# RetNet attention with a mixture-of-depths block on one core: twelve steps load k once and turn it on TensorE

## The chip, the core and the metric

The kernel runs on 1 core of one Trainium2 chip. The metric is the device time of one execution, in microseconds, as the median of the timed runs. The engines that appear below are TensorE (PE for its matmuls, PEld for its weight loads), VectorE (DVE), ScalarE (ACT), GpSimd (POOL) and SyncE (SP), whose queue issues nearly all transfers.

## The reference

Attention of the retention kind, for 8 batches, 8 heads, 576 positions and a head size of 64, all in float32:

```python
scores = scale * np.matmul(q, k.transpose(0, 1, 3, 2))
Dmat = np.where(rel >= 0, gamma[:, None, None] ** rel[None, :, :], 0.0)
ret = scores * Dmat[None, :, :, :]
return np.matmul(ret, v).astype(np.float32)
```

The result is regrouped to x with 8 x 576 rows of 512. Then, for each batch, the 128 rows with the largest score x·w_gate are taken, sent through a two-layer network (512 to 1024, ReLU, 1024 to 512), scaled by the sigmoid of their score and added to the row; the other rows stay as they are.

## The kernel before

**Attention by chunks.** The 576 positions of a batch are 9 chunks of 64. A step s takes two chunks, so the 8 batches make 36 steps; batch 0 is steps 0 to 4, with its ninth chunk in step 4. Half of the heads lie on partitions 0 to 63, the other half on 64 to 127, so matmuls of 64x64 run in pairs. For each step the host has packed a row of 2048 float32 a partition: q turned (head size on the partitions), k turned, v natural (positions on the partitions) and k natural. One transfer of 1 MB, `load`, brings them into a tile `raw` (8 buffers).

In step s TensorE makes, in `diagonal(s)`:
- u, the sum of k^T v over the chunks so far (`summed`): it takes k natural as the stationary operand and `vs`, v scaled by the decay, which POOL makes as soon as raw is there (`scaled`, 128x512);
- sc, the scores within a chunk: k turned against q turned.

and for the step before, in `crosswise(s - 1)`: y, from the masked scores am times vs, plus q turned times the state st of the chunk before. The generator `matmuls` takes two matmuls from each of the two lists in turn, so a step is about 16 such groups; the dictionary `inner` hangs further work in front of a given group. ACT copies u to st (`state`). `masked` multiplies sc by the causal mask on DVE. `values` scales y to xs: on ACT, in eight pieces of 128x64, for the steps in `BUSY`, and otherwise in one DVE instruction. `scored` makes the gate scores, `stored` writes xs out.

**Choice of rows and network.** `flatten`, `spread`, `compare` and `one_hot` find the rank of each row on DVE, with small matmuls in between; `fetch` gathers the chosen rows from the output by an indirect transfer of POOL (`xr`); `turn`, `up` and `down` are the network on TensorE (xg, h, ye). The pieces of the network of a batch are spread over the steps that follow its attention.

**What sets the order.** The order on each engine is the order of the program. Loads are put in it by `pe`: it counts TensorE's instructions (a float32 matmul is four, a transpose two), and at each edge of 256, where TensorE fetches its next block of instructions, it starts weights that are due (the list `due`, by step) and then raw loads, if fewer than 4 (in steps 4 to 6: 5) are ahead of the step. These transfers wait for the TensorE instruction at the edge. They go in order through the SP queue, together with the stores, which stand at the end of the steps that the dictionary `stores` names. A transfer in the queue that has to wait holds up all that is behind it.

For the prediction: "load s" is the load of step s, "vs(s)" the POOL instruction made from it, and "lead" the number of TensorE instructions between the edge that starts a load and the beginning of its step.

Of the kernel before, what the change touches and what calls it, by code (L numbers as in the profile page):

```python
# [10 lines left out]
F32 = mybir.dt.float32  # L11
# [6 lines left out]
P = 128  # L18
TINY = 2.0**-125
C = 64  # L20
# [19 lines left out]
def kernel(  # L40
# [37 lines left out]
    col = layout(NC, HG, cap)  # L78

    const = ctx.enter_context(tc.tile_pool(name="const", bufs=1))  # L80
    loads = ctx.enter_context(tc.tile_pool(name="loads", bufs=8))
    work = ctx.enter_context(tc.tile_pool(name="work", bufs=3))
    psum = ctx.enter_context(tc.tile_pool(name="psum", bufs=2, space=PSUM))

    def bank(name, tag="mm", bufs=3):
        return psum.tile([P, 512], F32, tag=tag, bufs=bufs, name=name)

    halves = [slice(0, C), slice(C, P)]

# [6 lines left out]
    raw, weights = {}, deque()  # L96
    now = {"at": BEFORE, "edge": BLOCK, "load": 0, "step": 0, "quiet": 0}

    def load(behind=None):
        s, now["load"] = now["load"], now["load"] + 1  # L100
        raw[s] = x = loads.tile([P, 4, DM], F32, name="raw")
        n = 4 if s else 2
        for a in range(0, 4, n):
            start(x[:, a : a + n, :],
                  qkvk[s, :, DM * a : DM * (a + n)].rearrange("p (a e) -> p a e", a=n), behind)

    def start(out, in_, behind):
        ins = nc.sync.dma_start(out=out, in_=in_)  # L108
        if behind is not None:
            tc.add_manual_dep(ins.ins, behind.ins.name, mybir.DependencyInfo(  # L110
                mybir.DependencyClass.Sync, mybir.DependencyReason.DATA), reason="behind a fetch")

    def pe(ins, n=4):

        now["at"] += n
        if now["at"] >= now["edge"] + SURE:
            now["edge"] += BLOCK
            lead = now["load"] - now["step"]
            if now["quiet"] and lead > 2:
                now["quiet"] -= 1  # L120
                return ins
            for _ in range(1 + (now["step"] > 8)):
                if weights and weights[0][0] <= now["step"]:
                    start(*weights.popleft()[1:], ins)

            ranks = (NC - 1) // 2 <= now["step"] < (NC - 1) // 2 + 3
            for _ in range(1 + (now["step"] == (NC - 1) // 2)):
                if now["load"] < NS and now["load"] - now["step"] < 4 + ranks:
                    load(ins)
        return ins  # L130
# [5 lines left out]
    def matmul(out, lhsT, rhs, **more):  # L136
        return pe(nc.tensor.matmul(out, lhsT, rhs, **more), 4 if lhsT.dtype == F32 else 2)  # L137
# [9 lines left out]
    load()  # L147
    w1_sb = const.tile([P, KD, F], F32, name="w1_sb")
    w2_sb = const.tile([P, FB, DM], F32, name="w2_sb")
    due = 5, 6, 8, 9, 9, 10, 10, 11  # L150
    assert FB == 8
    for i in range(FB // 2):
        e = slice(2 * P * i, 2 * P * i + 2 * P)
# [10 lines left out]
    eye = table[:, col["eye"] : col["eye"] + P]  # L164
# [5 lines left out]
    for _ in range(3):  # L170
# [7 lines left out]

    BUSY = range(1, (NC - 1) // 2 + 3)
    vs, am, sc_ps, y_ps, u_ps, st, xs, sc = {}, {}, {}, {}, {}, {}, {}, {}
    factor = lambda s, i: dec[:, i, chunk(s, 0)[1] : chunk(s, 0)[1] + 2, :].unsqueeze(3).to_broadcast(
        [P, 2, HG, D])

    def scaled(s):
        vs[s] = work.tile([P, DM], F32, name="vs", bufs=4)
        nc.gpsimd.tensor_tensor(out=four(vs[s]), in0=four(raw[s][:, 2, :]), in1=factor(s, 0),  # L188
                                op=OP.mult)

    def summed(s, a):

        b, c = chunk(s, a)
        if c == NC - 1:
            return
        if c == 0:
            u_ps[b] = bank("u_ps", "u", 1)
        for h in range(HG):
            for half in halves:
                yield lambda h=h, half=half: matmul(  # L200
                    u_ps[b][half, hd[0][h]], raw[s][half, 3, hd[a][h]], vs[s][half, hd[a][h]],
                    start=c == 0 and h == 0, stop=c == NC - 2, skip_group_check=True)
        state(s, a)

# [5 lines left out]
    def diagonal(s):  # L210

        if s:
            yield from summed(s, 0)
        sc_ps[s] = bank("sc_ps", "sc", 2)
        for a in range(2):
            for h in range(HG):
                for half in halves:
                    yield lambda a=a, h=h, half=half: matmul(
                        sc_ps[s][half, hd[a][h]], raw[s][half, 1, hd[a][h]],
                        raw[s][half, 0, hd[a][h]], start=True, stop=True, skip_group_check=True)  # L220
        masked(s)
        if s == 0:
            yield from summed(s, 0)
        yield from summed(s, 1)

    def crosswise(s):

        y_ps[s] = bank("y_ps", "y", 2)
        for a in range(2):
            for h in range(HG):  # L230
                for i, half in enumerate(halves):
                    yield lambda a=a, h=h, i=i, half=half: matmul(
                        y_ps[s][halves[1 - i], hd[a][h]], am[s][half, HG * a + h, :],
                        vs[s][half, hd[a][h]], start=a == 0 and h == 0, stop=chunk(s, a)[1] == 0,
                        skip_group_check=True)
        for a in range(2):
            b, c = chunk(s, a)
            if c == 0:
                continue
            for h in range(HG):  # L240
                for i, half in enumerate(halves):
                    yield lambda a=a, b=b, c=c, h=h, i=i, half=half: matmul(
                        y_ps[s][halves[1 - i], hd[a][h]], raw[s][half, 0, hd[a][h]],
                        st[b, c - 1][half, hd[0][h]], start=False, stop=True,
                        skip_group_check=True)

# [48 lines left out]
    def stored(s):  # L295
        (b, c), (b1, _) = chunk(s, 0), chunk(s, 1)
        for i, half in enumerate(halves):
            e = slice(W * i, W * i + W)
            if b == b1:
                nc.sync.dma_start(  # L300
                    out=outs[b][C * c : C * c + P, e].rearrange("(a t) e -> t a e", a=2),
                    in_=xs[s][half, :].rearrange("p (a e) -> p a e", a=2))
                continue
            nc.sync.dma_start(out=outs[b][C * c :, e], in_=xs[s][half, :W])
            nc.sync.dma_start(out=outs[b1][:C, e], in_=xs[s][half, W:])
# [128 lines left out]
    inner, first, soon, mid, late, then, ready, parts = {}, {}, {}, {}, {}, {}, [], deque()  # L434
# [11 lines left out]
    def plan(when, s, f, *a):  # L446
        when.setdefault(s, []).append((f, a))

    for b in range(B):
        end = cuts(b)  # L450
# [13 lines left out]
        s = there[-1]  # L464
# [28 lines left out]
        if b < B - 2:  # L493
# [3 lines left out]


    FETCH = (NC - 1) // 2 + 3
    stores = {4: [], 5: [0, 1, 2, 3], 6: [], FETCH: [], FETCH + 1: [], FETCH + 2: [5, 6],  # L500
              FETCH + 3: [7, 8], FETCH + 4: [9]}
    assert NC == 9
    scaled(0)
    scaled(1)
    for s in range(NS + 1):
        now["step"] = s
        now["at"] += 1.5
        if s == FETCH + 1:
# [109 lines left out]
```

## Time and profile before

| | |
|---|---|
| Time, median of 3 runs | 263.08 us (261.78 to 267.94) |
| Span of the profiled execution | 259.6 us |
| TensorE busy | 225.9 us, 87% |
| DVE, ACT, POOL busy | 154.5, 60.6, 59.3 us |
| Transfers | 56.95 MB, 219 GB/s on average |
| 35 raw loads of 1024 KB | median 7.9 us from issue to landing |
| 8 transposes of xg by four | 32 matmuls of 128x128, 5.4 us busy |

Busy time of TensorE counts matmuls that overlap in its pipeline once for the stretch that they cover. A wait is put down to what came last of what an instruction waited for. The table by step shown below gives for each stretch its length, the busy time of each engine with the number of instructions, the mean clock that TensorE was granted (1.00 is full), the busy share of the DMA engines and what they moved.

### The profile page before, as it was taken

The numbers are of one execution on the slowest core, as the hardware profiler recorded it, in microseconds if no ns is written. First come the engines' busy times: TensorE is split into PE (matmuls) and PEld (weight loads), VectorE is DVE, ScalarE is ACT, GpSimd is POOL, SyncE is SP. The second block draws the span as 40 slices with busy tenths as digits, with TensorE's granted clock in tenths as the row PEclk, the third lists the DMA queues.
The fourth block names the chain that finished last, engine by engine and source line by source line (L and its number), as shares of the span: only waits on it lengthen the run. The fifth ranks groups of instructions, "written<-read, shape, count | busy, mean of one in ns | idle before, by whom it ended". The sixth has DMA issues, their size and how long they took to land.

```text
span 259.6 us, 11383 instructions
## 1 busy us (share of the span) xinstructions
PE 225.9 (87%) x5104; PEld 176.5 (68%) x5104; DVE 154.5 (59%) x444; ACT 60.6 (23%) x183; POOL 59.3 (23%) x59
## 2 busy tenths in 40 slices
PE   8656657498879889987999998999999999999991
PEld 2554457498556679656996598677975995784940
DVE  0164994335796659966964499569983891950101
ACT  1146333024211232121221221122221220211200
POOL 3333321111033320223313221225131310101101
PEclk9999975789979999997999999999999999999999
DMA  6897996969998866885986674778977312111101
GB/s 207 337 323 252 368 274 193 370 234 315 409 344 262 246 248 190 242 277 194 337 267 232 223 249 144 262 251 257 302 247 276 107 47 78 43 40 40 43 0 42
DMA packets 20273, 56.95 MB, mean 219 GB/s; under 512 B 2304, under 2 KB 13696, under 8 KB 15744
## 3 DMA queue, kind: packets, MB, share of 16 engines
q1 hardware_dynamic: 18944, 52.02, 59.4%
q0 software_dynamic: 1280, 4.20, 5.0%
q8 instruction: 40, 0.66, 1.0%
q14 instruction: 9, 0.07, 0.1%
HBM read 44.67 MB, written 11.53 MB: 217 GB/s over the span
## 4 chain that ended last, share of the span: by engine, by line
PE 47%; issue 21%; DMA 20%; DVE 5%; POOL 4%; SPq 1%; POOLq 1%; ACT 0%; DVEq 0%
DMA raw<-in_qkvk 19%; PE h_ps L137 13%; PE ye_ps L137 10%; PE sc_ps L137 8%; PE u_ps L137 7%; PE y_ps L137 6%; POOL vs L188 3%; PE row_ps L137 2%; DVE scr L360 2%; DMA out<-xs 1%; PE xg_ps L404 1%; POOL xr L385 1%; DVE scr L292 1%; SPq L108 1%; DVE flat L321 1%
## 5 line engine op out<-in xcount | busy, mean ns | idle before, releaser
L188 POOL TENSOR_TENSOR vs<-raw,table 128x512 f32<-128x512 f32 x36 | 40.1, 1113 | 121.9 <-DMA raw<-in_qkvk 104.1
L137 PE MATMUL u_ps<-vs,raw 64*64 64x64 f32 x1024 | 46.4, 233 | 18.6 <-POOL vs L188 16.4
L137 PE MATMUL h_ps<-xg,w_sb 128*128 128x128 f32 x512 | 61.1, 278 | 1.1 <-issue 1.1
L137 PE MATMUL ye_ps<-w_sb,hT 128*128 128x512 f32 x128 | 61.2, 614 | 0.0
L137 PEld LDWEIGHTS h_ps<-xg,w_sb 128*128 128x128 f32 x512 | 58.6, 192 | 3.2 <-issue 2.2
L137 PEld LDWEIGHTS u_ps<-vs,raw 64*64 64x64 f32 x1024 | 38.8, 145 | 27.5 <-POOL vs L188 19.7
L261 DVE TENSOR_TENSOR am<-sc_ps,table 128x512 f32<-128x512 f32 x36 | 24.8, 689 | 43.7 <-PE sc_ps L137 27.1
L137 PE MATMUL y_ps<-vs,am 64*64 64x64 f32 x1152 | 46.3, 232 | 1.0 <-issue 1.0
L137 PE MATMUL sc_ps<-raw 64*64 64x64 f32 x1152 | 45.2, 230 | 0.2 <-DMA raw<-in_qkvk 0.2
L137 PEld LDWEIGHTS sc_ps<-raw 64*64 64x64 f32 x1152 | 41.0, 145 | 3.0 <-DMA raw<-in_qkvk 1.5
L208 ACT COPY st<-u_ps 128x256 f32<-128x256 f32 x64 | 23.9, 374 | 81.7 <-PE u_ps L137 54.4
L137 PE MATMUL y_ps<-st,raw 64*64 64x64 f32 x1024 | 41.2, 232 | 0.7 <-issue 0.7
L137 PEld LDWEIGHTS y_ps<-vs,am 64*64 64x64 f32 x1152 | 40.4, 143 | 1.9 <-issue 1.9
L292 DVE SCALAR_TENSOR_TENSOR scr<-xs,table 128x256 f32<-128x256 f32 x72 | 35.4, 492 | 8.0 <-ACT xs L277 5.7
L360 DVE SCALAR_TENSOR_TENSOR scr<-row,tok,ahead 128x576 f32<-128x576 f32 (+5 forms) x52 | 37.6, 723 | 2.9 <-ACT row L336 0.8
L137 PEld LDWEIGHTS y_ps<-st,raw 64*64 64x64 f32 x1024 | 37.6, 148 | 0.9 <-issue 0.8
L137 PEld LDWEIGHTS ye_ps<-w_sb,hT 128*128 128x128 f32 x128 | 23.1, 193 | 22.0 <-issue 20.6
L280 DVE TENSOR_TENSOR xs<-y_ps,table 128x512 f32<-128x512 f32 x30 | 20.5, 682 | 8.2 <-PE y_ps L137 8.0
L416 ACT ACTIVATE hT<-h_ps 128x256 f32<-128x256 f32 x32 | 12.3, 384 | 50.2 <-PE h_ps L137 50.2
L428 DVE SCALAR_TENSOR_TENSOR o<-ye_ps,gate,xr 128x512 f32<-128x512 f32 x8 | 6.0, 749 | 26.3 <-PE ye_ps L137 13.5
L353 DVE SCALAR_TENSOR_TENSOR scr<-row,table 128x128 f32<-128x128 f32 (+1 forms) x40 | 13.2, 331 | 10.5 <-ACT row L336 9.8
L429 POOL DMA_INDIRECT out<-o,idx x8 | 8.6, 1070 | 43.0 <-DVE o L428 32.8
(33 smaller groups left out, 110.9 us busy)
## 6 DMA issues: line engine op xcount, KB each, us to landing
raw<-in_qkvk SPq DMA_DIRECT2D x35, 1024.0 KB, 7.9
out<-xs SPq DMA_DIRECT2D x64, 128.0 KB, 6.4
w_sb<-in_w SPq DMA_DIRECT2D x8, 512.0 KB, 7.0
raw<-in_qkvk SPq DMA_DIRECT2D x2, 512.0 KB
out<-xs SPq DMA_DIRECT2D x16, 64.0 KB, 5.5
table<-in_consts SPq DMA_DIRECT2D x1, 258.5 KB, 8.2
wg<-in_w_gate SPq DMA_DIRECT2D x1, 256.0 KB
xr<-out,idx POOLq DMA_INDIRECT x8, 6.5
```

The costliest lines, as they stand in the source:

```text
L108: ins = nc.sync.dma_start(out=out, in_=in_)
L137: return pe(nc.tensor.matmul(out, lhsT, rhs, **more), 4 if lhsT.dtype == F32 else 2)
L188: nc.gpsimd.tensor_tensor(out=four(vs[s]), in0=four(raw[s][:, 2, :]), in1=factor(s, 0), op=OP.mult)
L208: nc.scalar.copy(out=st[b, c], in_=u_ps[b][:, :W])
L261: nc.vector.tensor_tensor(out=am[s], in0=sc_ps[s].rearrange("p (h d) -> p h d", h=H), in1=causal.unsqueeze(1).to_broadcast([P, H, C]), op= ...
L280: nc.vector.tensor_tensor(out=four(xs[s]), in0=four(y_ps[s]), in1=factor(s, 1), op=OP.mult)
L292: nc.vector.scalar_tensor_tensor(scr[:, :W], part, 1.0, wg_half, op0=OP.mult, op1=OP.mult, accum_out=sc[b][:, c : c + 1])
L353: nc.vector.scalar_tensor_tensor(scr[:, :n], row[b][:, P * j : P * j + n], 1.0, eye[:, :n], op0=OP.mult, op1=OP.mult, accum_out=tok[b][:, ...
L360: nc.vector.scalar_tensor_tensor(scr[:, : i1 - i0], row[b][:, i0:i1], tok[b][:, j : j + 1], ahead[:, at + i0 : at + i1], op0=OP.subtract, ...
L416: nc.scalar.activation(out=hT[b][:, f : f + n, :], in_=t[:, :n, :], func=AF.Relu)
L428: nc.vector.scalar_tensor_tensor(o, ye[b], gate[b], xr[b], op0=OP.mult, op1=OP.add)
L429: nc.gpsimd.indirect_dma_start(out=outs[b], out_offset=bass.IndirectOffsetOnAxis(ap=idx[b][:, :1], axis=0), in_=o, in_offset=None)
```

## The change

In steps 2 to 13 (`NAT`) the natural form of k is no longer loaded: a load of these steps is 768 KB. TensorE makes it from k turned, with four transposes of 128x128 for each of the two chunks, and ACT copies each four from PSUM to a new tile `nat`. So that one transpose of 128x128 gives both halves of the heads in their places, the host packs k and q turned side by side, with the rows of partitions 64 to 127 rotated by 64 elements; `turned` finds a block in it. The purpose is to move fewer bytes while the weights are also being loaded.

Around it the order is changed: ACT makes xs only in steps 4 to 6, DVE does in 1 to 3; the second piece of weights is due in step 8 rather than 6, two pieces are allowed at an edge from step 8 on; at the edge in step 6 two loads start, and the stores of step 4 come after them, at the end of step 6.

```diff
+    NAT = range(2, 14)
...
+        raw[s] = x = loads.tile([P, 4 * DM], F32, name="raw")
+        end = 3 * DM if s in NAT else 4 * DM
+        n = 2 * DM if s == 0 else end
+        for a in range(0, end, n):
+            start(x[:, a : a + n], qkvk[s, :, a : a + n], behind)
+
+    def turned(s, part, a, h, i):
+        at = D * ((2 * HG * part + HG * a + h + i) % (4 * HG))
+        return raw[s][halves[i], at : at + D]
...
-            for _ in range(1 + (now["step"] > 8)):
+            for _ in range(1 + (now["step"] > 7)):
...
-            for _ in range(1 + (now["step"] == (NC - 1) // 2)):
+            for _ in range(1 + (now["step"] in ((NC - 1) // 2, (NC - 1) // 2 + 2))):
...
-    due = 5, 6, 8, 9, 9, 10, 10, 11
+    due = 5, 8, 8, 9, 9, 10, 10, 11
...
-    BUSY = range(1, (NC - 1) // 2 + 3)
+    BUSY = range((NC - 1) // 2, (NC - 1) // 2 + 3)
...
+    def natural(s):
+        nat[s] = work.tile([P, 2, HG, P], F32, name="nat", bufs=2)
+        for a in range(2):
+            t = bank("nat_ps").rearrange("p (h e) -> p h e", h=HG)
+            for h in range(HG):
+                at = W * a + D * h
+                pe(nc.tensor.transpose(t[:, h, :], raw[s][:, at : at + P], eye), 2)
+            nc.scalar.copy(out=nat[s][:, a, :, :], in_=t)
...
-                    u_ps[b][half, hd[0][h]], raw[s][half, 3, hd[a][h]], vs[s][half, hd[a][h]],
+                    u_ps[b][half, hd[0][h]],
+                    nat[s][half, a, h, half] if s in NAT else raw[s][half, 3 * DM :][:, hd[a][h]],
+                    vs[s][half, hd[a][h]],
...
-    stores = {4: [], 5: [0, 1, 2, 3], 6: [], FETCH: [], FETCH + 1: [], FETCH + 2: [5, 6],
+    stores = {4: [], 5: [0, 1, 2, 3], 6: [4], FETCH: [], FETCH + 1: [], FETCH + 2: [5, 6],
...
+    for s in NAT:
+        plan(inner, (s - 1, 9), natural, s)
...
-            stored(s - 1)
...
+    kq = np.concatenate([turned(k), turned(q)], axis=2)
+    kq[:, C:] = np.roll(kq[:, C:], C, axis=2)
+    packed = np.concatenate([kq, natural(v), natural(k)], axis=2)
```

More of the change, by code (lines that the diff above doesn't have):

```diff
@@ L100, in load @@
         s, now["load"] = now["load"], now["load"] + 1
[L101 to L105, printed above, removed]
+        raw[s] = x = loads.tile([P, 4 * DM], F32, name="raw")
[6 more added lines that the diff above has]
+        return raw[s][halves[i], at : at + D]
     def start(out, in_, behind):
@@ L187, in scaled @@
         vs[s] = work.tile([P, DM], F32, name="vs", bufs=4)
-        nc.gpsimd.tensor_tensor(out=four(vs[s]), in0=four(raw[s][:, 2, :]), in1=factor(s, 0),
+        nc.gpsimd.tensor_tensor(out=four(vs[s]), in0=four(raw[s][:, 2 * DM : 3 * DM]), in1=factor(s, 0),
                                 op=OP.mult)
+    nat = {}
+    def natural(s):
[6 more added lines that the diff above has]
+            nc.scalar.copy(out=nat[s][:, a, :, :], in_=t)
     def summed(s, a):
@@ L216, in diagonal @@
             for h in range(HG):
[L217 to L220, printed above, removed]
+                for i, half in enumerate(halves):
+                    yield lambda a=a, h=h, i=i, half=half: matmul(
+                        sc_ps[s][half, hd[a][h]], turned(s, 0, a, h, i), turned(s, 1, a, h, i),
+                        start=True, stop=True, skip_group_check=True)
         masked(s)
@@ L242, in crosswise @@
                     yield lambda a=a, b=b, c=c, h=h, i=i, half=half: matmul(
-                        y_ps[s][halves[1 - i], hd[a][h]], raw[s][half, 0, hd[a][h]],
+                        y_ps[s][halves[1 - i], hd[a][h]], turned(s, 1, a, h, i),
                         st[b, c - 1][half, hd[0][h]], start=False, stop=True,
@@ L576 @@
     q, k, v = inputs["q"], inputs["k"], inputs["v"]
-    packed = np.stack([turned(q), turned(k), natural(v), natural(k)], axis=2)
+    kq = np.concatenate([turned(k), turned(q)], axis=2)
+    kq[:, C:] = np.roll(kq[:, C:], C, axis=2)
+    packed = np.concatenate([kq, natural(v), natural(k)], axis=2)
     col = layout(NC, HG, cap)
```

## The prediction

> **What bounds the kernel now.** I read the page first, then who waited for whom, then the waits of TensorE alone, a table of the span by step, and the SP queue in order of time. Slices are 6.5 us.
>
> ```profile
> PE 225.9 (87%) x5104; PEld 176.5 (68%) x5104; DVE 154.5 (59%) x444; ACT 60.6 (23%) x183; POOL 59.3 (23%) x59
> ...
> PE   8656657498879889987999998999999999999991
> ...
> PEclk9999975789979999997999999999999999999999
> DMA  6897996969998866885986674778977312111101
> ```
>
> TensorE stands at 8 or 9 (once 7) from the 13th slice (78 us) on, but at 4 to 8 in nearly all slices before, and there its clock falls as well, while the DMA engines stand mostly at 8 or 9. So there are two stretches: one fed too slowly, then one bound by TensorE to the end. Of TensorE's waits:
>
> ```profile
> PE u_ps L137 <- POOL vs L188: 16.4, 12, 3.5
> PE idx_ps L137 <- DVE hot L370: 3.1, 1, 3.1
> PE row_ps L137 <- DVE flat L321: 2.1, 2, 1.5
> ```
>
> and behind the first stands POOL's own wait for the loads of raw (104.1 us, 28 times): POOL scales v in 1.04 us as soon as a load lands. The table by step (length, PE busy, PEld, DVE, ACT, POOL, granted clock, DMA share, GB/s):
>
> ```profile
> 14.50:18.20 3.70, 2.05 (x128) 1.91 (x129) 1.83 (x6) 1.99 (x9) 1.04 (x1) 1.00 0.96 334
> 35.50:43.30 7.80, 4.19 (x133) 3.87 (x133) 5.53 (x21) 2.51 (x12) 2.53 (x2) 0.72 0.70 223
> 43.30:50.40 7.10, 3.63 (x112) 3.52 (x112) 3.11 (x10) 1.86 (x9) 1.04 (x1) 0.74 0.94 323
> 50.40:58.30 7.90, 7.85 (x162) 7.15 (x163) 2.05 (x5) 1.66 (x4) 1.04 (x1) 0.80 0.73 270
> 66.40:72.80 6.40, 3.98 (x133) 2.60 (x132) 5.97 (x17) 1.19 (x4) 1.04 (x1) 1.00 1.03 401
> 72.80:78.00 5.20, 5.17 (x132) 3.72 (x133) 5.03 (x14) 0.74 (x2) 1.03 (x1) 0.67 0.96 327
> 118.30:200.00 81.70, 80.94 (x1975) 64.60 (x1976) 58.68 (x168) 18.42 (x51) 21.82 (x20) 0.98 0.75 247
> ```
>
> A step's own matmuls take 2.05 us at full clock (first row). Steps 7 and 8 take over 7 us each: half idle, half at a low clock. Over all rows up to 72.8 us TensorE is busy 50.5 us, idle 22.3. From 72.8 to 118.3 it is idle 4.8, from there to 200 only 0.8. Why load 9 is late is seen in the SP queue:
>
> ```profile
> 29.24 0.57 SPq L108 DMA_DIRECT2D raw<-in_qkvk  x1
> 29.90 7.88 SPq L300 DMA_DIRECT2D out<-xs  x8
> 37.88 0.62 SPq L304 DMA_DIRECT2D out<-xs  x1
> ...
> 40.51 0.60 SPq L108 DMA_DIRECT2D w_sb<-in_w  x1
> 41.22 1.46 SPq L108 DMA_DIRECT2D raw<-in_qkvk  x1
> ```
>
> Its edge on TensorE came at about 33 us (an estimate from its place in step 6), but twelve stores and a weight load stand ahead of it; it issues at 41.22, vs(9) starts at 49.36, and TensorE stands from 46.98 to 50.45. Load 12 (60.55, behind two weight loads) is used at 71.73 and costs 2.45 us (70.38 to 72.83); load 20 (108.37) costs 2.25 us at 116.07.
>
> **What the Trainium skill says.** "TensorE: Matmul & The Clock Gate", Part 1: the clock is gated by a monitor with windows of 3.4 us, and is at half after an idle window, and the rule given is to have no idle gap over 3.4 us. The trace agrees in kind, but is stricter: the clock is 0.50 in 34 to 36 us, 40 to 44 and 50.4 to 52, and the waits of 2.45 and 2.25 us too were followed by a dip (0.67 above). Same page, Part 4: a transpose on TensorE took about 275 ns in one kernel, and doesn't count as busy for the monitor. Here the xg transposes last 273 ns each, but pipelined four take 0.44 us on the chain; whether they count, no row shows. "DMA: Bandwidth & Descriptors", Issuing engines are not separate DMA queues: all transfers share 16 engines and interleave. The trace agrees: a 1 MB load alone is used 4.98 us after issue (load 3), load 12 behind 1 MB of weights 11.2 us.
>
> **The change part by part.**
>
> *Bytes removed.* Twelve loads carry 768 KB and not 1 MB: 12 x 0.26 = 3.1 MB less. At the 323 to 401 GB/s of the rows with a DMA share above 0.9, that is 8 to 10 us of DMA time, all of it before 70 us.
>
> *TensorE added.* 8 transposes a step in twelve steps, 96 of them, at 0.11 us: 0.88 a step, 10.6 in all at full clock (double at half: four took 1.04 us at 52.01). They sit in the middle of step s-1 and need raw[s] landed there, where before only u(s) at the start of step s did, after POOL. The 7 of 16 groups that follow take 7 x 0.117 = 0.8 us, in which POOL makes vs(s). From landing to step s is thus 0.9 + 0.8 = 1.7 us instead of 1.1.
>
> *ACT and DVE.* 24 copies of 128x512 at 0.587 (the xg row) are 14.1 us on ACT. The first is done about 1.2 us after its transposes begin, the u matmuls come 1.7 after: hidden. xs of steps 1 to 3 goes from ACT (1.76 a step) to DVE (0.68): ACT ends at about 69 us busy of 260; the chain y, xs, score, flat, rank loses about 1 us a step. The PSUM banks of the new tile come from the three of h_ps and row_ps; those copies are done within 2 us, so I give this nothing, with 0.3 us a step as the high end.
>
> *Queue moved.* At step 5's end 8 stores rather than 12; at step 6's edge loads 9 and 10 together, then the stores of step 4; the second weight piece moves from step 6 to 8, and issues in step 9. Nothing loads in steps 7 and 8. POOL's gather for batch 0 waits for those stores, and vs(9) is queued behind it on POOL.
>
> *Along the steps* (start before, my estimate after):
> - Steps 1 to 5: a period of two steps is edge offset + landing + landing-to-use. Before: 1.0 + 5.5 + 1.1 = 7.6 (load 4: issue 15.41, vs 20.88; load 5: 19.23, 24.83). After, with 0.75 MB landing in about 4.5: 0.8 + 4.5 + 1.7 = 7.0. Over four steps about 1 us: step 5 at 25.9 becomes 25.0. The transposes fill the waits.
> - To idx in step 7 DVE is the bound: from flat at 26.73 to hot at 39.8 it is nearly without a gap. It starts about 1.5 us sooner: 39.9 becomes 38.3. The idle time in front of idx stays in part, so I leave the half clock after it in.
> - Loads 9 and 10 issue at 32 to 34 us and land, with load 8, one weight piece and 8 stores ahead (3.75 MB from 25.5 at 300 GB/s), at about 38 to 39. The wait of 3.47 us goes. Steps 7 (rest 2.2) and 8 (3.1) run partly at half clock: step 9 at 47 (50.45). The gather goes out at about 44; its issues take 6.5 us to land by the median of the page, in empty queues less; xg starts between 48.7 and 50.5, and I take 48.7 (52.0 before).
> - Step 9 after xg: 0.44 + 1.1 + 0.9 + two h groups of 1.95 = 6.3: step 10 at 55.0 (58.7).
> - Step 10: 7.7 before, less a wait of 0.7, plus 0.9: step 11 at 62.9 (66.4).
> - Step 11: 6.46, less 2.45, plus 0.9: step 12 at 67.8 (72.8).
> - Step 12: 6.7, less 1.7 for the clock dip (5.2 x 0.33), plus 0.9: step 13 at 73.7 (79.5).
> - Steps 13 and 14 have no transposes and lose waits of 0.34 and 0.89, as loads 14 and 15 have some 190 TensorE instructions more of lead: step 15 at 81.6 (88.7), 7.1 us ahead.
> - DMA from step 9 on: L11, L12, L13, L14, L15 stand 1.75, 3.5, 5.75, 7.75, 9.0 MB behind its start; at 320 GB/s with 1.5 us latency they land at 54, 59.5, 66.5, 73, 76.7, each before its use above, with about 1 us to spare for 13.
> - Load 20 gets 526 instead of 333 instructions of lead: its wait of 2.25 goes, and the clock loss after it (0.02 x 81.7 = 1.6): 11 us ahead. Loads 22 and later mostly have 64 fewer (about 0.9 us); the smallest slack there is 0.83 us (load 30), so at most 0.5 is given back. The tail after 200 us is unchanged.
>
> Sum: 7.1 + 2.25 + 1.6 - 0.5 = 10.4. I take off 0.8 for waits that new instructions bring: 9.6, so 263.1 - 9.6 = 253.5 us.
>
> **Rivals.**
> 1. *The supply is only half mended.* Steps 1 to 8 keep their length (DVE chain, latency), the half-clock windows stay because of the waits in mid-step, the gather or load 13 is late. For it: 9 us without a load in steps 7 and 8, the thin margin of load 13. Against: 190 instructions more lead. Gain about half, 4 to 5: 258.5.
> 2. *TensorE becomes the bound at once*, and the transposes are paid in full: 10.6 us, 1.5 more at half clock, and 0.3 a step for copies and banks (3.6), 15.7 in all, against load waits after 46 us of 9.4 (3.47 + 2.45 + 2.25 + 0.34 + 0.89): 6 slower, 269. For it: 87% busy. Against: 22.3 us idle just where the transposes are put, and more idle time and half clock than they cost.
> 3. *More than forecast*: the clock never drops, since TensorE is busier in steps 5 to 8; 4 to 5 us more are saved: 248.5.
>
> **How the numbers follow.** Forecast 0.56, rival 1 0.22, rival 2 0.12, rival 3 0.10. Faster by over 2% (below 257.8): the forecast, rival 3 and a small part of rival 1, 0.71; within 2%: most of rival 1, 0.17; slower 0.12. The range, 247.5 to 261.5, takes in rivals 3 and 1 and the copies' 0.3 a step.
>
> **What would show it.** Right: transposes at about 0.11 us pipelined; no TensorE wait over 1 us from 47 to 75 us; load 9 issued before 35 us; step 15 at about 82; no wait near 110. Wrong: waits of the transposes for raw in steps 8 to 12; a clock still near 0.7 in 45 to 75 us; u matmuls waiting for the ACT copy; a gap at load 13 or 30.

## The result, and the profile after

The changed kernel takes 275.64 us (median of 4 runs, 274.36 to 278.62), the kernel before beside it 263.53 (4 runs, 261.78 to 267.94): ratio 1.0467, 95% interval 1.0372 to 1.0561. It is slower by 12 us, where 9.6 us of gain were forecast. Three later runs of the same program, on three chips, gave ratios of 1.0331 (1.0226 to 1.0435) and 1.0398 (1.0315 to 1.0481) and, without an interval, 271.57 us against 264.80. Ratios are taken from undisturbed runs alone and medians from all runs, so the two can differ by some us. The kernel before itself takes 259.5 to 266.0 us from chip to chip, so times below are compared only on one chip.

From the page of the kernel after: busy time by engine, the span in slices of 6.8 us, and a line of the queues (packets, MB, share of the engines' time).

```profile
PE 242.7 (89%) x5200; PEld 187.1 (69%) x5200; DVE 156.1 (57%) x447; ACT 68.3 (25%) x183; POOL 58.7 (22%) x59
...
PE   8779658999988999479999999979999999999991
...
PEclk9999995799999999977999999999999999999997
...
q8 instruction: 41, 0.67, 1.0%
```

From the eighth slice (48 us) on TensorE stands at 8 or 9: the weak stretch has become shorter at its end, as forecast. But there are new holes behind it, a 4 in the 17th slice (109 to 116 us) and 7s in the 18th and 27th, where the kernel before had at least 8; and the low clock in the 18th and 19th is two slices long, where it was one. TensorE's waits in the kernel after (what waited, for what, total us, times, longest):

```profile
PE y_ps L143 <- issue: 7.6, 10, 3.5
PE u_ps L143 <- issue: 3.6, 4, 1.7
PE u_ps L143 <- ACT st L228: 3.4, 7, 0.6
PE idx_ps L143 <- DVE hot L390: 2.8, 2, 2.7
...
PE u_ps L143 <- POOL vs L194: 1.3, 2, 0.7
```

The wait that the change was made against, u for vs, fell from 16.4 us to 1.3. In its place stand 12.0 us of waits for "issue" (7.6 + 3.6 + 0.8 for sc; 3.9 before): nothing that the profile knows as a releaser, no semaphore and no transfer of the program. The table by step of the kernel after (length, PE busy, PEld, DVE, ACT, POOL, granted clock, DMA share, GB/s):

```profile
14.60:18.40 3.80, 3.27 (x136) 2.91 (x137) 2.13 (x7) 1.82 (x4) 1.04 (x1) 1.00 0.49 176
...
37.30:46.80 9.50, 6.18 (x141) 5.26 (x141) 5.10 (x21) 3.59 (x15) 0.46 (x1) 0.66 0.68 221
...
73.20:81.20 8.00, 6.96 (x211) 5.06 (x214) 7.30 (x20) 1.98 (x5) 2.19 (x3) 1.00 1.00 355
...
108.30:126.80 18.50, 13.02 (x262) 8.24 (x261) 7.54 (x22) 2.00 (x6) 4.53 (x4) 0.82 0.52 171
```

and the same work as in its last row, steps 18 and 19, in the kernel before:

```profile
106.70:118.30 11.60, 9.14 (x258) 6.34 (x257) 9.42 (x23) 2.45 (x7) 3.67 (x3) 1.00 0.91 296
```

First row: TensorE is now 3.27 of 3.80 us busy in a step that took 3.70 before with 2.05 busy; the DMA share fell from 0.96 to 0.49. The step has changed its limit and kept its length. Last rows: 6.8 us (by the exact starts below) are lost in steps 18 and 19 alone, where the change touches nothing, with the DMA engines at half load. Where time was lost follows from the start of u in some steps:

| start of u(s), us | 5 | 9 | 13 | 15 | 18 | 20 | 28 | 31 | 35 |
|---|---|---|---|---|---|---|---|---|---|
| before | 25.93 | 50.45 | 79.53 | 88.67 | 106.68 | 118.33 | 167.76 | 184.29 | 209.85 |
| after | 26.11 | 51.38 | 81.18 | 89.90 | 108.34 | 126.77 | 176.24 | 195.41 | 222.82 |
| later by | 0.2 | 0.9 | 1.7 | 1.2 | 1.7 | 8.4 | 8.5 | 11.1 | 13.0 |

So there are two questions: why the first 13 steps gained nothing, and what happens from step 18 on. TensorE's instructions in order of time, in the kernel after, show one moment of each (start, duration, what it waited for in brackets):

```profile
14.60 0.27 PE L143 MATMUL u_ps<-vs,nat 64*64 64x64 f32 x2 [0.56 <-ACT st L228]
...
15.81 1.09 PE L206 MATMUL nat_ps<-table,raw 128*128 128x128 f32 x8
16.83 0.27 PE L143 MATMUL sc_ps<-raw 64*64 64x64 f32 x2
...
110.08 0.23 PE L143 MATMUL u_ps<-vs,raw 64*64 64x64 f32 x2
113.82 0.27 PE L143 MATMUL y_ps<-st,raw 64*64 64x64 f32 x2 [3.51 <-issue]
```

At 110.3 TensorE stops in the middle of a row of equal matmuls, all of whose operands are there. The page's queue of instructions says what it can be waiting for: 41 packets of 16 KB, one for about 256 TensorE instructions (the page has 5200 records of matmuls and 5200 of weight loads; a float32 matmul stands there as two of each). The packets of that queue around this place start at 97.53, 103.65, 111.39 and 119.55 us: TensorE stands until 1.5 us after the third has landed (112.34), and then again for 1.74 us, until 1.4 us after the fourth has (120.50). The kernel's loads are started at the edges of just these blocks. The SP queue of the kernel after:

```profile
98.44 0.33 SPq L114 DMA_DIRECT2D raw<-in_qkvk  x1
98.87 1.29 SPq L320 DMA_DIRECT2D out<-xs  x2
102.18 4.72 SPq L114 DMA_DIRECT2D raw<-in_qkvk  x2
106.99 1.44 SPq L320 DMA_DIRECT2D out<-xs  x2
114.25 0.33 SPq L114 DMA_DIRECT2D raw<-in_qkvk  x1
```

Loads 18, 19, 20 (98.44, 102.18, 106.57) are 3.7 and 4.4 us apart, and 21 follows one block on; in the kernel before the three take 9.5 us from first to last (98.89 to 108.37), here 8.1. **Theory A**: 96 transposes of two instructions are 192, so from step 14 on the grid of 256 stands 64 instructions away from where it stood against the steps; loads now fall together in blocks that TensorE passes quickly, and instruction blocks come late. **Rival B**: transposes, copies and the new order cost what they cost, and the late waits are theirs or chance.

### The profile page after: what moved, and what is told of

The parts are those of the page before. It is cut to its first block, busy times and chain, and to the rows that moved or that the text cites. A ratio compares the mean times of both kernels' runs of the same rounds, so it can differ in the third digit from the quotient of the medians.

```text
span 272.7 us, 11572 instructions
## 1 busy us (share of the span) xinstructions
PE 242.7 (89%) x5200; PEld 187.1 (69%) x5200; DVE 156.1 (57%) x447; ACT 68.3 (25%) x183; POOL 58.7 (22%) x59
## 2 busy tenths in 40 slices
DMA packets 20274, 53.82 MB, mean 197 GB/s; under 512 B 2304, under 2 KB 13696, under 8 KB 17280
## 4 chain that ended last, share of the span: by engine, by line
PE 57%; issue 24%; DVE 8%; DMA 7%; POOL 2%; SPq 1%; POOLq 1%; ACT 0%; DVEq 0%
PE h_ps L143 14%; PE ye_ps L143 12%; PE sc_ps L143 9%; PE u_ps L143 8%; PE y_ps L143 7%; DMA raw<-in_qkvk 5%; PE nat_ps L206 4%; DVE scr L380 3%; PE row_ps L143 3%; DMA out<-xs 2%; DVE scr L373 1%; DVE scr L312 1%; PE xg_ps L424 1%; POOL xr L405 1%; DVE am L281 1%
## 5 line engine op out<-in xcount | busy, mean ns | idle before, releaser
L143 PE MATMUL ye_ps<-w_sb,hT 128*128 128x512 f32 x128 | 62.5, 625 | 0.0
L143 PE MATMUL y_ps<-vs,am 64*64 64x64 f32 x1152 | 46.9, 228 | 3.6 <-issue 3.2
L143 PE MATMUL sc_ps<-raw 64*64 64x64 f32 x1152 | 48.0, 226 | 1.0 <-issue 0.8
L143 PE MATMUL y_ps<-st,raw 64*64 64x64 f32 x1024 | 41.9, 223 | 4.6 <-issue 4.4
L143 PEld LDWEIGHTS y_ps<-vs,am 64*64 64x64 f32 x1152 | 39.7, 139 | 4.5 <-issue 3.7
L143 PEld LDWEIGHTS y_ps<-st,raw 64*64 64x64 f32 x1024 | 36.0, 138 | 5.3 <-issue 5.3
L143 PE MATMUL u_ps<-vs,raw 64*64 64x64 f32 x688 | 30.4, 224 | 5.3 <-issue 3.6
L143 PEld LDWEIGHTS u_ps<-vs,raw 64*64 64x64 f32 x688 | 24.7, 136 | 11.9 <-issue 8.3
L300 DVE TENSOR_TENSOR xs<-y_ps,table 128x512 f32<-128x512 f32 x33 | 22.6, 683 | 13.3 <-PE y_ps L143 13.0
L373 DVE SCALAR_TENSOR_TENSOR scr<-row,table 128x128 f32<-128x128 f32 (+1 forms) x40 | 14.3, 359 | 14.1 <-ACT row L356 13.3
## 6 DMA issues: line engine op xcount, KB each, us to landing
table<-in_consts SPq DMA_DIRECT2D x1, 258.5 KB, 7.4
```

The costliest lines, as they stand in the source:

```text
L300: nc.vector.tensor_tensor(out=four(xs[s]), in0=four(y_ps[s]), in1=factor(s, 1), op=OP.mult)
L373: nc.vector.scalar_tensor_tensor(scr[:, :n], row[b][:, P * j : P * j + n], 1.0, eye[:, :n], op0=OP.mult, op1=OP.mult, accum_out=tok[b][:, ...
```

## The experiments

**Restore the grid (e1).** The changed kernel with 16 small matmuls more, 64 instructions, in step 13, so that 256 are added in all and the grid is back in place; nothing else is touched.

```diff
+    def filler(n):
+        t = bank("idle_ps")
+        for _ in range(n):
+            matmul(t[:C, :C], ones[:C, :C], ones[:C, :C], start=True, stop=True)
+    plan(inner, (13, 2), filler, 16)
```

> The changed kernel with 16 small matmuls (64 TensorE instructions, about 0.5 us) added in step 13, so that all that follows stands at the same place in the grid of 256 instructions as in the kernel before (192 + 64 = 256). Theory A (the loss after step 18 comes from the shift of that grid against the steps: loads start in a bunch, and TensorE's instruction fetch is stuck behind them): the waits for issue near 110, 120 and 180 us go, about 264 us, 11 less than the changed kernel. Theory B (the loss comes from the transposes and the new order themselves, whatever the grid): about 276 us.

Measured: 259.63 us (20 runs), the kernel before on this chip 259.64 (39 runs); ratio 1.003 (0.9984 to 1.0077). Its waits:

```profile
PE u_ps L143 <- ACT st L228: 3.4, 7, 0.6
PE idx_ps L143 <- DVE hot L390: 2.8, 2, 2.6
...
PE u_ps L143 <- issue: 1.9, 1, 1.9
...
PE h_ps L143 <- issue: 0.6, 2, 0.4
```

More work, and the loss is gone within the interval. The waits for issue fell from 12.0 to 3.0 us, and loads 18 to 20 take 11.4 us from first to last. The filler was expected to take about 0.5 us; in the trace it takes 2.74 (78.55 to 81.29), partly at half clock.

**Displace the grid of the kernel before (e2), and displace it by a whole block (h1).** The kernel before with the same filler in step 13: 48 matmuls (192 instructions) in e2, 64 (256) in h1.

> The kernel before with 48 small matmuls (192 TensorE instructions, about 1.4 us) added in step 13 and nothing else: the same shift of the grid as in the changed kernel, with no transposes, no smaller loads and the old order. Theory A: it loses what the changed kernel lost after step 18, and comes to 274 to 277 us. Theory B: 263.5 + 1.4, about 265 us.

> The kernel before with 64 small matmuls in step 13: 256 instructions, so the grid of fetches stands as before from there on, where 48 of them (192) displaced it and cost 15 us. Theory A (the displacement costs, not the number of instructions): the padding's own 64 x 0.11 = 7 us at most, less the load waits of steps 13 to 20 that it gives time for: 4 to 8 slower than the kernel before, and no wait for issue over 2.5 us behind step 13. Rival B (added instructions cost by themselves): a third more than the 15 us of 48, 18 to 21 slower.

Measured: e2 275.05 us (4 runs, 266.34 to 281.24) against 259.64, so 15.4 slower by medians; no ratio is on record, but its lowest run lies above all but one of the 39 runs of the kernel before. h1 266.12 (259.53 to 271.39) against 259.46, ratio 1.0228 (1.0076 to 1.038): 6.7 slower by medians, 5.8 by the ratio. Adding more costs less than half as much by medians, if it is a whole block. The waits of e2

```profile
PE u_ps L137 <- POOL vs L188: 9.6, 8, 2.0
PE u_ps L137 <- issue: 8.4, 5, 4.5
```

hold one of 4.48 us at 112.75 to 117.23, six steps behind the filler, where a packet of instructions starts at 114.93 and lands at 115.85; those of h1

```profile
PE u_ps L137 <- issue: 1.7, 3, 0.6
...
PE y_ps L137 <- issue: 0.8, 1, 0.8
```

hold none over 0.8. Rival B falls, and with e1 this shows in both kernels that the place of the blocks sets the loss. The filler's own price was set too low in both expectations: its 48 matmuls take 5.60 us in e2 (75.21 to 80.81), 0.117 each, so some 10 of the 15.4 us are left for the displacement. By the same price the 64 of h1 make 7.5 us (an estimate from e2), which is all of its loss; in its profiled execution, the slowest of six, they took 11.8 us, mostly at half clock.

**The bytes without the transposes (e3), the order without the bytes (e4).** e3 is the changed kernel without `natural`, so its grid is not displaced; u takes v in place of the natural form of k in steps 2 to 13, so that part of u is left out. e4 has only the new order: every load has 1 MB and no k is turned.

```diff
-    for s in NAT:
-        plan(inner, (s - 1, 9), natural, s)
...
-                    nat[s][half, a, h, half] if s in NAT else raw[s][half, 3 * DM :][:, hd[a][h]],
+                    raw[s][half, (2 if s in NAT else 3) * DM :][:, hd[a][h]],
```

```diff
-    NAT = range(2, 14)
+    NAT = range(2, 2)
```

> The changed kernel without the transposes and their copies: loads of steps 2 to 13 stay at 768 KB and the new order stays; the u matmuls of these steps read natural v where natural k would stand, so this part of the sum is left out of the computation. The grid is that of the kernel before. It measures what the smaller loads and the order are worth without TensorE's price. Theory A: waits for loads before 75 us shrink and nothing is lost later, 252 to 256 us. Rival: the early steps are bound by the chain from u over the ACT copy to the next u, or by DVE, and not by the loads: 260 to 264 us.

> The changed kernel with no step in the list of turned steps: all loads 1 MB, no transposes, but the new order (xs on DVE in steps 1 to 3, two loads at step 6's edge, the stores of step 4 behind them, weights later). Theory A: loads 9 and 10 in time take away the wait of 3.47 us and one stretch of half clock, about 258 us. Rival: the MB moved are the bound, and what comes earlier for load 9 comes later for 11 to 13: 262 to 265 us.

Measured, on the chip of e1: e3 254.80 us, ratio 0.9917 (0.984 to 0.9995); e4 260.46, ratio 1.0142 (1.002 to 1.0263). In e3

```profile
PE u_ps L143 <- POOL vs L194: 6.9, 5, 2.3
PE idx_ps L143 <- DVE hot L390: 4.1, 2, 3.5
```

and in e4

```profile
PE u_ps L143 <- POOL vs L194: 8.9, 7, 2.1
PE xg_ps L424 <- DMA xr<-out,idx: 3.8, 2, 3.6
```

By medians the steps are: order +0.8 (e4 less before), bytes -5.7 (e3 less e4), transposes with 16 filler matmuls +4.8 (e1 less e3), and that is nothing in all. By the ratios they are +3.7, -5.8 and +2.9, so only the bytes' share is firm. In e4 the waits for vs are already down from 16.4 to 8.9, but idx comes hardly sooner (39.48 after 39.86), and the gather, which waits for step 4's stores behind loads 9 and 10, costs xg 3.56 us: the rival's time came true. The time of e3 lies in theory A's range only because this chip is faster; as a gain on the kernel before, 4.8 us (2.2 by the ratio) is less than the 7.5 to 11.5 of theory A and nearer to the rival, for which the early steps are bound by DVE or by the chain through ACT. The bytes alone are worth 5.7 us, where 9.6 were forecast for the whole.

**Fill a wait, and turn only where loads are short (f3, f4).** f3 puts the 16 filler matmuls (of 64x1) in front of idx in step 7, where TensorE waits 2.65 us for hot. f4 does so too, with 40 of them, and turns k in steps 8 to 13 only.

```diff
+    plan(inner, (7, 4), filler, 16)      # f3; f4: 40
...
-    NAT = range(2, 14)                   # f4
+    NAT = range(8, 14)
```

> The changed kernel with 16 small matmuls ahead of idx in step 7, where TensorE waits for hot anyway (2.65 us); they bring the added instructions from 192 to 256. Theory A: from step 8 on the grid stands as in the kernel before, the late waits for issue are gone, and the padding costs nothing: 257 to 260, up to 2 less than with the padding in step 13 (259.6). If the filled wait also keeps the clock up, the half clock from 40 us on shrinks from 6.8 to 10 us to 3.4 or less and the time is 254 to 256. Rival B (the place in step 13 mattered, not the count): the waits near 110 return, over 268.

> k is made by TensorE in steps 8 to 13 alone (96 instructions), steps 2 to 7 load it again, and 40 small matmuls ahead of idx in step 7 bring the sum to 256. Theory A with 'the transposes of steps 2 to 5 only take the place of the load waits': steps 1 to 5 are as in the kernel before (flat near 26.8, idx near 40), 4.8 us of transposes less than with all twelve, some of it given back by later loads in 6 to 8: 255 to 259. Rival C (the smaller loads of steps 2 to 7 are what keeps the supply going): loads 9 to 13 come late again, waits of POOL for vs of over 3 us in all, 261 or more.

Measured: the kernel before took 264.80 us on this chip, f3 265.20, ratio 1.0055 (1.0006 to 1.0103), f4 266.39, ratio 1.0086 (1.0017 to 1.0154). The chip is some 5 us slower than that of the expectations, so only differences count. f3 is 0.4 (by medians) to 1.5 us slower than the kernel before: no wait for issue is over 0.8 us, as theory A said, but nothing is gained. The half clock behind the wait stayed, later: by the table of f3 the granted clock was 1.00 in 36 to 42 us, 0.79 in 42 to 48, 0.50 in 48 to 52 and 0.54 in 52 to 56, which makes 10.2 us of half clock (2.5 + 4 + 3.7), as long as in the changed kernel and longer than in e1 (6.8), and not the 3.4 that was hoped for. In f4

```profile
PE u_ps L143 <- POOL vs L194: 8.6, 4, 3.6
```

waits of 3.56 and 3.09 us stand at the start of steps 3 and 5, where the kernel before waits 1.65 and 1.59; loads 3 and 5 took 7.5 and 6.9 us to land there, and why is open. f4 was expected 1 to 5 us below the kernel before and is 1.6 above: theory A's gain failed, the rival's time came true, though its waits are not those of loads 9 to 13. Six steps' transposes less bought nothing, which fits the reading that in steps 2 to 5 transposes only took the place of waits, and doesn't prove it.

**What of st (g2)?** Of the changed kernel's waits, 3.4 us are u's for st, seven of about 0.55. If they come because ACT is busy copying nat, sooner transposes remove them.

```diff
-        plan(inner, (s - 1, 9), natural, s)
+        plan(inner, (s - 1, 4), natural, s)
...
+    plan(inner, (7, 4), filler, 16)
```

> The changed kernel with the 16 small matmuls ahead of idx in step 7, and the transposes of a step in its 5th group and not in its 10th, 0.6 us sooner. Theory: TensorE's seven waits of 0.55 for st (3.1 us) come because ACT copies nat (2 x 0.53) when st is wanted; sooner, they are gone: 1.5 to 3 us less than the padded kernel, 1 us or more under the kernel before. Rival: the loads haven't landed that soon (slack 1.3 to 2.5 us in steps 3 to 7 is used up), transposes wait for raw, and the gain is under 0.5 or a loss.

Measured: 271.78 us against 265.97, ratio 1.0285 (1.0175 to 1.0395). In its waits

```profile
PE y_ps L143 <- issue: 6.6, 11, 2.4
PE u_ps L143 <- issue: 4.0, 2, 3.6
PE u_ps L143 <- ACT st L228: 3.8, 7, 0.6
```

those for st are as before the edit, so my theory of them falls. Turning back to the order of time shows it: in the kernel after ACT is free when the last u of a step is done (14.04), copies st from 14.09 to 14.46, and u of the next step starts at 14.60, because it adds to the same PSUM bank. This chain was there before, hidden in the longer wait for vs. The rest is the grid again: the transposes now stand at another place of the blocks in steps 1 to 12, and waits for issue of 3.56 (31.37) and 2.42 us (51.62) appear where there were none.

**Is it the bytes (f1, f2), the stores (h2, h3), or the order of load and fetch (g1, g3)?** f1, g3 and h3 are the changed kernel itself, as references on their chips. f2 cuts the loads of steps 16 to 35 to 768 KB too (u takes v for k there: that part of u is left out). h2 holds the stores of steps 15 to 17 until after step 19. g1 starts each load 32 instructions further behind its edge.

```diff
-        end = 3 * DM if s in NAT else 4 * DM
+        end = 3 * DM if s in NAT or s > 15 else 4 * DM                # f2
...
-                    nat[s][half, a, h, half] if s in NAT else raw[s][half, 3 * DM :][:, hd[a][h]],
+                    nat[s][half, a, h, half] if s in NAT else raw[s][half, (2 if s > 15 else 3) * DM :][:, hd[a][h]],
...
-              FETCH + 3: [7, 8], FETCH + 4: [9]}
+              FETCH + 3: [7, 8], FETCH + 4: [9], 17: [], 18: [], 19: [15, 16, 17]}   # h2
...
-SURE = 8
+SURE = 40                                                            # g1
```

> The changed kernel itself, once more, as the reference for the others of this call. Theory A (192 more TensorE instructions displace the grid of 256-instruction fetches against the steps; fetches then come late behind bunched loads and stores): the waits for issue on TensorE are where they were, 3.5 us near 110, 1.7 near 120, 1.3 near 180, and the time is 274 to 277. Rival B (those waits were chance of one execution): they are elsewhere or smaller, and the time is nearer 265.

> The loads of steps 16 to 35 carry 768 KB too, and u takes v in place of the natural form of k in those steps (that part of u is left out); no instruction of TensorE is added or moved, so the grid stays displaced. Theory A in the form 'a fetch waits behind the bytes of bunched loads': the waits of 3.5, 1.7 and 1.3 us near 110, 120 and 180 fall below 0.7 each, their two half-clock windows go, and the time falls by 8 to 11 from the changed kernel's, to about 265. Rival B (the displaced grid makes the fetch late by itself, bytes or not: because of the order of edges, semaphores or stores): the waits stay within a third of their size and the time stays over 271.

> The changed kernel itself, for the spread of its times and as the reference of the next one. Theory A' (a fetch of instructions and the packets of a load and stores race for the DMA engines; on the displaced grid the fetch loses in some executions and not in others): times spread over 8 us or more, and the profile shows single waits for issue of 1 to 4 us in blocks with a load and stores in the one before, not all where they were. Rival B (a fixed cost of the displaced grid): the spread is that of the kernel before, and the waits stand where they stood.

> The changed kernel with each load issued 32 TensorE instructions further behind the edge of its block (SURE 40 and not 8), about 0.9 us later, all else as it is. Theory A': the fetch gets its packets in ahead of the load more often: waits for issue over 1 us go, the spread shrinks, and the median falls by 4 to 10 from the changed kernel's on the same chip, less up to 2 for loads that come 0.9 later. Rival C (the fetch waits because loads are bunched in short blocks, whichever is first): the waits and the median stay, or get 1 to 2 worse.

> The changed kernel itself, as the reference of the next one on the same chip. Theory: waits for issue of 3 to 4 us near 110 and of 1.2 near 178, in most executions, and 7 to 13 us over the kernel before.

> The changed kernel with the twelve stores of steps 15 and 16 (and 17) held until after step 19, where a block has no load; TensorE's instructions and the loads are untouched. Theory A (the fetch near 106 stands behind the bytes of loads 19 and 20 and of the 0.25 MB of stores right behind load 20): with the stores gone from there, the wait of 3.5 us near 110 shrinks to under 1.5 and the time falls by 2 to 5 from the changed kernel's, the other waits staying. Rival D (the loads alone hold it, stores don't matter): the wait of 3.5 stays and the time is within 1.5 of the changed kernel's.

Measured: f1 271.57 us (266.60 to 277.04) and f2 267.90 (263.14 to 272.93) against 264.80, f2's ratio 1.0089 (1.004 to 1.0137); g3 272.09 and g1 271.85 against 265.97, g1's ratio 1.0318 (1.0243 to 1.0394); h3 266.54 and h2 267.75 against 259.46, h2's ratio 1.048 (1.0346 to 1.0614).

The surprise is f1. Its profiled execution took 266.60 us, 8 less than the first profile of the same program, and its waits for issue are small:

```profile
PE y_ps L143 <- issue: 3.0, 8, 0.6
...
PE u_ps L143 <- issue: 2.3, 3, 1.3
```

So these late blocks are not a fixed cost of the displaced grid. From the packets of the instruction queue in each trace one can count how many of TensorE's records precede each packet. All seven kernels below have the same TensorE program, so the earliest place at which a packet starts in any of them says when it is due, and the rest is its delay:

```
us late, packet due     after   f1     g3     h3     h2     f2     g1
behind load 20          4.43   0.36   4.90   0.35   0.41   0.37   1.36
behind load 21          4.82   0.76   3.98   4.93   4.63   0.33   2.24
behind load 29          3.10   3.09   3.21   3.16   3.17   2.19   0.41
```

In the kernels other than g1 the first two are due 0.4 to 1.1 us behind the issue of a load. They start within 0.8 us, or 4.0 to 4.9 us later; nothing lies between. In f1 both were on time, in h3 one, in the first profile none. The third, due 2.5 us behind a load, is 3.1 to 3.2 us late in all kernels but f2 and g1, so not all is chance. What each edit did:
- h2: no change beside h3. Both have the second packet late and the first on time (a wait of 3.50 at 112.45, and of 3.78 at 113.68); the stores are not it.
- f2: the first two are on time, but so they are in f1, which has full loads, so this says nothing of the bytes. In its one trace the third is 0.9 us less late than in the five others, and the median is 3.7 below f1's; the expected 8 to 11 was too much, since another packet, at load 22, is 4.3 us late there and a wait of 1.53 us stays.
- g1: neither of the first two is more than 2.3 us late, and the third is on time, but another is late (4.2 us, behind load 23), and a wait of 2.23 us comes at 84. The median stays: rival C was right on the time.

What is shown: with the grid in its old place from step 14 on (before, e1, e3, e4, f3, f4, h1) no wait for issue is over 1.9 us; with it displaced (after, f1, f2, g1, g3, h2, h3, e2) five of eight traces have one of 3.5 to 4.5, each ending 1.3 to 1.7 us after a packet of instructions has landed. What decides in one execution whether a packet is late is open. That the bytes of bunched loads hold them up fits loads 18 to 20 (8.1 us from first to last in the kernel after, 8.0 in e2, 9.5 to 11.4 in the kernel before, e1 and f3) and the third packet of f2, and is not settled: the spacing is the same in f1, where the first two packets were on time. It speaks against a plain shortage of bandwidth that the DMA engines were only partly busy while the first packet was due, by the table of the kernel after:

```profile
106.00:108.00 2.00, 1.94 (x10) 0.98 (x10) 1.43 (x2) 0.00 (x0) 0.84 (x1) 1.00 0.56 156
108.00:110.00 2.00, 2.00 (x113) 1.66 (x115) 1.90 (x8) 0.37 (x1) 0.20 (x1) 1.00 0.73 270
110.00:112.00 2.00, 0.31 (x21) 0.18 (x12) 1.43 (x2) 0.00 (x0) 1.45 (x1) 1.00 0.91 329
```

None of the versions beats the kernel before; e3, which does, leaves work out.

## Why the prediction was wrong

**Bytes removed: right in size, and smaller in effect.** 3.1 MB less moved (56.95 to 53.82 MB). Forecast were 8 to 10 us of DMA time, all before 70 us; e3 against e4 puts it at 5.7 us of the span.

**TensorE added: the step that was under-priced.** Transposes run pipelined as forecast, eight in 1.02 us from the first to the next matmul's start (15.81 to 16.83) against 0.88. The failure is in "the transposes fill the waits". In steps 1 to 5 they do, but only as far as to replace them: 2.05 us of own work, 1.22 more with the transposes (3.27 busy) and 0.55 of the u, st, u chain make the step of 3.8 us, where the forecast had 7.0 for two. In its terms, edge offset and landing were right: loads 3 to 5 landed in 4.4 to 4.6 us (4.5 forecast). From landing to the start of the step 1.7 us were forecast and 2.7 (load 3: 15.72 to 18.43) and 2.5 (load 5: 23.61 to 26.11) measured, since the rest of a step took longer than 0.8 us and the wait for st came on top. vs was ready 1.3 to 1.6 us before u could use it in steps 2, 3 and 5, but no slack was left for the transposes: in steps 2 to 5 they started 0.05 to 0.3 us after the load had landed, once (20.03) after a wait for it. Step 5 began at 26.11 and not at 25.0. Over all steps the transposes, with e1's filler, took back 2.9 to 4.8 of the bytes' 5.7 us (e1 and e3).

**ACT and DVE: the copies are hidden, the chain is not sooner.** No matmul waits for a copy of nat, and g2 shows that the waits for st don't come from these copies. But flat started at 27.64 (26.73 before) and idx at 41.24 (39.86), where 38.3 was forecast; e3, without transposes, had idx at 40.34, so they are not what holds it. The wait in front of idx was left in the forecast as it was; it is 2.65 us, and half clock lasts from 40.3 to 50.5, 10.2 us, where there were 6.8 from 40.0 on. Its length changes by execution: 6.8 us in g3 and h2, 10.2 in f1 and h3, with the same TensorE program. There the 8 transposes of steps 8 and 9 took 1.97 and 1.83 us, not 0.88.

**Queue moved: right in kind, 2 to 4 us late.** The SP queue of the kernel after:

```profile
27.52 0.56 SPq L114 DMA_DIRECT2D raw<-in_qkvk  x1
28.17 7.71 SPq L320 DMA_DIRECT2D out<-xs  x8
35.98 1.03 SPq L114 DMA_DIRECT2D raw<-in_qkvk  x2
```

Loads 9 and 10 issue at 35.98 and 36.62 (41.22 and 46.05 before), forecast were 32 to 34: the eight stores ahead of them still take 7.71 us. The wait of 3.47 us for vs(9) went, as forecast. The gather went out at 46.34 and not at 44. idx had been there since 41.8; it waited for the stores of step 4, which the new order puts behind loads 9 and 10: those loads landed at 41.11 and 44.79 and not at 38 to 39, the stores at 44.97 to 45.52. The gathered rows landed at 50.69, and xg came at 52.93 (52.0 before) and not at 48.7, because TensorE reached it no sooner.

**Steps 9 to 13: the sizes of single steps were near, but for step 12.** From the start at 51.38 instead of 47, step 9 took 8.8 us (8.0 forecast), 10 7.9 (7.9), 11 5.1 (4.9), 12 8.0 (5.9), of which 1.04 idle. The clock dip of the kernel before was counted in step 12 as 1.7 us to be gained and was worth half of that: without it the step's other work is still 5.9 us (6.96 busy less 1.1 of transposes), where it was 6.70. Loads 11 to 13 landed at 60.9, 68.8 and 74.4, not at 54, 59.5 and 66.5, with the DMA share at 0.93 to 1.00, and only 0.1 to 0.5 us before their transposes. Of the signs named as right, transposes at about 0.11 us and no wait over 1 us from 47 to 75 us are there, and the clock is 1.00 from 50.5 to 75; load 9 before 35 us (35.98), step 15 at about 82 and no wait near 110 (3.51) are not. Step 15 began at 89.90, not at 81.6: of the 8.3 us, 1.1 arose to step 5, 3.3 more to step 9, 3.1 more to step 13, 0.8 to step 15.

**Load 20 and the rest: the step that failed outright.** "Load 20 gets 526 instead of 333 instructions of lead: its wait of 2.25 goes, and the clock loss after it" was counted at 3.85 us of gain, less 0.5 for loads with 64 instructions fewer. The count of instructions was right, and it was used only for when loads land. That the same count moves the edges, and with them which blocks hold a load and how closely loads follow each other, was before my eyes in the same numbers, and I priced it at nothing. Measured: two packets of instructions 4.4 and 4.8 us late, waits of 3.51 and 1.74 us, and 6.8 us lost from step 18 to 20 and 4.5 from there to step 35, where 3.35 were to be gained; with the grid put back (e1) the loss is gone. The rest of the 13.0 us at step 35 is the 1.7 with which step 18 began.

**The rivals.** Rival 2 came nearest in time (269) and for the wrong reason: its transposes and copies were to cost 15.7 us against 9.4 of load waits, and e1, which has them all, takes as long as the kernel before. Without the displaced grid, rival 1 (258.5, 4.6 gained) would have been nearest, and still too good by all of its gain. Its reason held for the first 50 us: steps 1 to 8 kept their length (step 9 at 51.38 after 50.45), and the half clock stayed. No case in the list had the grid in it; all of them argued about steps 2 to 13.

**The clock and the shared engines.** In the Trainium skill, "TensorE: Matmul & The Clock Gate", Part 1, gives the rule of no idle gap over 3.4 us. This case is stricter again: TensorE has no wait longer than 2.65 us up to idx, and in that wait half clock sets in (40.3), for 10.2 us. "DMA: Bandwidth & Descriptors", Issuing engines are not separate DMA queues, says that transfers of all issuing engines share 16 engines. The page of the profile counts the instruction packets' time as a share of 16 engines too; that fits their delays of 4 to 5 us behind loads, though no run here shows where they stand.

## What to carry to other kernels

If a kernel ties its transfers to a count of instructions, an edit that adds instructions moves every later transfer, also in steps that it doesn't touch: work out the shift modulo the block, look where transfers fall together, and try the edit once with padding to a whole block before judging it. Work that fills a wait gains nothing by itself, and shorter transfers gain nothing where the filler takes all that they free: the new length of such a step here was the new sum on TensorE, with a chain that the old wait had hidden. A wait for "issue" in the middle of equal, ready instructions is worth comparing with the packets of the instruction queue.

## What the runs showed of the hardware

TensorE's instructions come as packets of 16 KB, one for about 256 instructions, 0.9 to 1.8 us each; the page counts them among the transfers of the DMA engines. TensorE stops when one is late and goes on 1.3 to 1.7 us after it has landed (113.82 after 112.34 in the kernel after, 112.43 after 111.15 in g3, 115.95 after 114.23 in h2); the profile names no releaser for it. The two packets behind loads 20 and 21 were, in one program, either under 1 us late or 4.0 to 4.9, by execution. The changed kernel spread from 266.6 to 277.0 us on one chip, but so wide a spread has the kernel before there too (259.6 to 271.6), so it isn't shown to come from this. Small matmuls of 64x64 cost 0.117 us each at full clock (48 in 5.60 us in e2), so even padding isn't free. Transposes of 128x128 run at 0.11 us from start to start at full clock, eight in 1.83 to 1.97 us at half.
